# An attention block's backward pass: dWq and dWmod by whole rows through V's buffers

## The chip, the cores and the metric

The kernel runs on one core of a Trainium2 chip. The metric is the device time of one execution in microseconds; the median of three runs before the change is 1378.13 us (1377.52 to 1378.75).

The core has five engines that run at the same time: TensorE (PE) multiplies matrices into PSUM, VectorE (DVE) and ScalarE (ACT) do elementwise work and sums, GpSimd (POOL) and SyncE (SP) here mainly issue DMA transfers. Sixteen DMA engines move data between HBM and the on-chip SBUF, which has 128 partitions. A DMA transfer is split into packets; where a tile takes a contiguous run of bytes for each partition, the run is a packet.

## The reference

The reference computes one decode step of a transformer block (one token, D = 640, 32 heads of width 192, 8192 cached positions) and all of its gradients with respect to the inputs, the caches and most of the weights. Cut to what matters:

```python
mod = (silu(c) @ w_mod).reshape(1, 6, 1, 640)        # sa, ca, ga, sb, cb, gb
h = layernorm(x) * (1 + ca) + sa
q = (h @ wq).reshape(...)                            # wq: 640 x 6144
p = softmax(einsum(q, k) * 192 ** -0.5); o = einsum(p, v)
x = x + ga * (o @ wo)
h = layernorm(x) * (1 + cb) + sb
x = x + gb * B(h)                                    # a small MLP block
out, vjp = jax.vjp(f, x, k_cache, v_cache, wq, wo, w3, w4, c, w_mod)
grads = vjp(grad_out)
```

All arrays are bf16. The caches are 32 x 8192 x 192, so K, V, dK and dV are 100.7 MB each. The forward pass reads K and V, the backward pass reads V again and writes dK and dV. Two of the smaller gradients are the subject here. With dq (6144 values) and the input ha of the projection (640 values), dWq is the outer product ha x dq (640 x 6144), and the gradient of ha is Wq times dq, which sums each row of Wq weighted with dq. In the same way dWmod = silu(c) x dmod (640 x 3840), and Wmod times dmod goes into the gradient of c.

## The kernel before

A head's K or V is held as two tiles of 128 partitions x 32 positions x 192 values: 12,288 contiguous bytes for each partition, 1.5 MiB in all. The forward pass goes through the heads with a buffer set of its own. The backward pass runs in the order of heads HS (31 down to 0), in a loop over `i` (L1251) that emits, for each head:

- the side jobs of list `J0[i]`;
- `bwd_mult` for both halves: VectorE multiplies V by the broadcast gradient (L132), TensorE sums the products with an identity matrix into PSUM (L1018). From iteration 21 on this is done one head ahead;
- `ring_load` (L751): loads of V for later heads;
- for the next head, dV: ScalarE writes 20 of 32 positions of each half (L1023, one instruction each), VectorE the other 12 (L1001); stores on SyncE's queue (L1026);
- the side jobs of list `J1[i]`, then dS (`bwd_ds`) and dK for both halves on VectorE (L1001), with stores on SyncE's queue (L1053);
- the side jobs of list `J2[i]`.

So an iteration moves two tiles of V in, and two of dV and two of dK out: 9.44 MB. Each engine works in the order in which the program was written (`pin_order` fixes it for TensorE, VectorE and ScalarE); SyncE issues transfers in program order too, and a transfer whose data or buffer isn't ready holds all that are behind it. The program gives SyncE's transfers eight semaphores in turn, so at most eight of them are under way.

Buffers: dV and dK take tiles from `big`, five tiles in turn (`big_order`), and from iteration 25 (`I_SIDE` = 24) seven, with two tiles x and y that lie where the side jobs' pools were. V lives in a ring of six slots (`NR`), filled in the order of the list `ring`: two halves per head, and four batches of Wo early on. The load of entry n is emitted when entry n - 6 has been consumed.

The side jobs touched by the change compute dWq, dWmod and the two weighted row sums. Before, Wq is cut into four pieces of 1536 columns (`QG`) and Wmod into three of 1280 (`MG`), by `add_outer`; each piece takes two iterations:

- `job_outer_load` (L1114) loads all 640 rows of a piece, as 128 partitions x 5 blocks x 1536 or 1280 columns, on SyncE's queue;
- `job_outer_bc` broadcasts the piece of dq or dmod to all partitions: TensorE multiplies with the identity, four blocks of 128 at a time (L191), ScalarE copies from PSUM (L195);
- `job_outer_mul` multiplies on VectorE (L132) and sums on TensorE into 5 x 96 or 5 x 80 columns of PSUM with 16 matmuls (L1129);
- `job_outer_red` finishes the sum on VectorE (L1134 to L1138);
- `job_outer_out`, once for each of five row blocks, scales the broadcast by a column (`tsc`: ScalarE for even blocks, L1068, VectorE for odd ones, L1070) and stores 128 x 1536 or 128 x 1280 on SyncE's queue (L1143).

Wq's pieces are loaded at iterations 9, 11, 13, 15 and worked two iterations later, Wmod's at 17, 19, 21. `job_x0` (iteration 18) turns the finished sum into dx and into the first two parts of dmod, and `job_c` (iteration 24) makes the gradient of c. Their pools are `in` (one buffer), `out` (four) and `bc` (one).

Of the kernel before, what the change touches and what calls it, by code (L numbers as in the profile page):

```python
# [20 lines left out]
def kernel(  # L21
# [26 lines left out]
    nc = tc.nc  # L48
# [45 lines left out]
    def bank(tag, bufs=1, name=None, n=512):  # L94
        return psum[0].tile([P, n], FP32, tag=tag, name=name or "ps_" + tag, bufs=bufs)
# [35 lines left out]
    def mul(out, a, b):  # L131
        nc.vector.tensor_tensor(out=out, in0=a, in1=b, op=ALU.mult)  # L132

    def add(out, a, b):
        nc.vector.tensor_tensor(out=out, in0=a, in1=b, op=ALU.add)
# [50 lines left out]
    def bcast_cols(col_bf, c0, n, out_bc, evac, ps_in=None):  # L186
        for g0 in range(0, n, 4):
            g1 = min(n, g0 + 4)
            ps = ps_in if ps_in is not None else bank_c("bc_ps")
            for k in range(g0, g1):  # L190
                nc.tensor.matmul(ps[:, (k - g0) * P : (k - g0 + 1) * P], lhsT=col_bf[:, c0 + k : c0 + k + 1].to_broadcast([P, P]), rhs=ident_bf, start=True, stop=True)  # L191
            evac(out_bc[:, g0 * P : g1 * P], ps[:, 0 : (g1 - g0) * P])
# [135 lines left out]
    def load_v(pool, h, t, slot, eng=None):  # L328
        tl = pool.tile([P, JH, DH], BF16, name="V_sb", tag=f"v{slot}")
        (eng or nc.sync).dma_start(out=tl, in_=V_hd[h][:, t * JH : (t + 1) * JH, :])  # L330
        return tl
# [196 lines left out]
    def flat(tl):  # L528
        return tl.rearrange("p j d -> p (j d)")
# [206 lines left out]
    wo_b = {}  # L736
    WS = 32
    BATCHES = [(2, 3, 4), (5, 6, 7), (8, 9, 10), (11, 12, 13), (14, 15)]
    ring = []
    for i in range(1, HQ):  # L740
        ring += [("v", HS[i], t) for t in range(2) if (i, t) != (1, 1)]
        if i % 2 == 1 and 0 < i // 2 < len(BATCHES):
            ring.append(("w", i // 2, 0))
    ring_n, freed = [0], set()
    ldq = nc.sync
    NR = 6
# [4 lines left out]
    def ring_load():  # L751
        while ring_n[0] < len(ring) and (ring_n[0] < 3 or ring_key(ring_n[0] - NR) in freed):
            n = ring_n[0]
            kind, k, t = ring[n]
            slot = ring_slot(n)
            pool = bv if slot > 2 else fv
            ring_n[0] += 1
            if kind == "v":
                V_b.setdefault(k, {})[t] = load_v(pool, k, t, slot, ldq if n >= 3 else nc.sync)
            else:  # L760
                load_wo(k, pool.tile([P, JH, DH], BF16, name="V_sb", tag=f"v{slot}"))

    def load_wo(k, tl):
        lo, n = PS[BATCHES[k][-1]], len(BATCHES[k])
        tl = tl.rearrange("p j d -> p (j d)")[:, 0 : 3 * n * D].rearrange("p (c r) -> p c r", r=D)
        wo_b[k] = tl
        nc.gpsimd.dma_start(out=tl, in_=wo_v[:, 3 * lo : 3 * (lo + n), :])
# [341 lines left out]
    dha_c = ccol(NDC, "dha_c")  # L1109
    dsc_c = ccol(NDC, "dsc_c")  # L1110

    def job_outer_load(name, view, lo, n):
        w = side["in"].tile([P, NDC, n], BF16, name=name, tag="win")
        ldq.dma_start(out=w, in_=view[:, :, lo : lo + n])  # L1114
        side[name, lo] = w

    def job_outer_bc(name, lo, n, col_bf):
        v_bc = side["bc"].tile([P, n], BF16, name=name + "_bc", tag="vbc")
        bcast_cols(col_bf, lo // P, n // P, v_bc, act_copy)
        side[name + "_bc"] = v_bc  # L1120

    def job_outer_mul(name, lo, n):
        w = side.pop((name, lo))
        mul(w, w, side[name + "_bc"][:, None, :].to_broadcast([P, NDC, n]))
        ps = bank("b", name="js_ps")
        NS = 16
        W = n // NS
        for k in range(NS):
            nc.tensor.matmul(ps[:, 0 : NDC * W].rearrange("p (i w) -> p i w", w=W), lhsT=ident_bf, rhs=w[:, :, k * W : (k + 1) * W], start=(k == 0), stop=(k == NS - 1))  # L1129
        side[name + "_ps"] = ps[:, 0 : NDC * W].rearrange("p (i w) -> p i w", w=W)  # L1130

    def job_outer_red(name, acc, first):
        if first:
            nc.vector.reduce_sum(out=acc, in_=side[name + "_ps"], axis=AX.X)  # L1134
        else:
            red = bsm.tile([P, NDC], FP32, name="red")
            nc.vector.reduce_sum(out=red, in_=side[name + "_ps"], axis=AX.X)
            add(acc, acc, red)  # L1138

    def job_outer_out(name, lo, n, i, rows_f, dram):  # L1140
        o = side["out"].tile([P, n], BF16, name=name + "_o", tag="wout")
        tsc(o, side[name + "_bc"], rows_f[:, i : i + 1], i)
        st2.dma_start(out=dram[i * P : (i + 1) * P, lo : lo + n], in_=o)  # L1143

    def job_x0():
        dmod_sa, dmod_ca = dmod_c[:, 0:NDC], dmod_c[:, NDC : 2 * NDC]
# [14 lines left out]
        mul(sp, sp, dsc_c)  # L1161
        store_cols(out_8[0], sp, const, st2, "dco")

    QG = QD // 4
    MG = NMOD // 3
    NPH = 10
    J0, J1, J2 = [{i: [] for i in range(HQ)} for _ in range(3)]
    for k in range(HH):
# [3 lines left out]
    for k in range(NDC):  # L1172
        J1[5 + HH + k].append(lambda i=k: job_dw3(i))

    def add_outer(at, name, view, lo, n, col_bf, rows_f, dram, acc, first):
        J2[at].append(lambda: job_outer_load(name, view, lo, n))
        J0[at + 2].append(lambda: job_outer_bc(name, lo, n, col_bf))
        J1[at + 2].append(lambda: job_outer_mul(name, lo, n))
        J2[at + 2].insert(0, lambda: job_outer_red(name, acc, first))
        for i in range(NDC):  # L1180
            (J2[at + 2] if i < 3 else J1[at + 3]).append(lambda i=i: job_outer_out(name, lo, n, i, rows_f, dram))

    for g in range(4):
        add_outer(NPH - 1 + 2 * g, "wq", wq_v, g * QG, QG, dq_bf, ha_f, out_4, dha_c, g == 0)
    for k, g in enumerate((1, 2, 0)):
        add_outer(NPH + 7 + 2 * k, "wm", wm_v, g * MG, MG, dmod_bf, sc_f, out_9, dsc_c, k == 0)
    J2[NPH + 8].append(job_x0)
    J2[NPH + 14].append(job_c)

    wo_first = [(PS[1], cc) for cc in range(3)]  # L1190
# [60 lines left out]
    for i in range(HQ):  # L1251
        h, nxt = HS[i], HS[i + 1] if i + 1 < HQ else None
        if i % 2 == 1 and i > NPH and nxt is not None:
            bwd_dob(nxt // 2)
        for f in J0[i]:
            f()
        if i <= AHEAD:
            if i in SPLIT:
                bwd_pf(nxt)
            for t in range(2):  # L1260
                bwd_mult(h, t, 2 if i == 0 else 1)
                if i == t == 0:
                    ring_load()
                    c_first = fin_c(PS[0], 1)
                if i in SPLIT:
                    bwd_dv(nxt, t)
        if i not in EARLY:
            ring_load()
        if i - 1 in dq:
            fin_dq(*dq.pop(i - 1))  # L1270
        if i == 0:
            fin_c_copy(PS[0], 1, c_first)
        if nxt is not None and i not in SPLIT:
            if i > 0:
                bwd_pf(nxt)
            for t in range(0 if i > 0 else 1, 2):
                bwd_dv(nxt, t)
        if i in EARLY:
            ring_load()
        if i == 0:  # L1280
            bwd_ds(h)
            dq_last(h)
        if i < NPH:
            hook(i)
        if i == 3:
            bcast_cols(du_bf, 0, NFC, du_bc, act_copy)
        for f in J1[i]:
            f()
        if i > 0:
            bwd_ds(h)  # L1290
        if i >= AHEAD and nxt is not None:
            for t in range(2):
                bwd_mult(nxt, t)
        bwd_dk(h, 0)
        bwd_dk(h, 1)
        if i in cps:
            fin_c_copy(*cps.pop(i))
        if i == 1:
            mid_cols()
            job_mid()  # L1300
            dve_copy(dmod_bf[:, 2 * NDC : 6 * NDC], dmod_c[:, 2 * NDC : 6 * NDC])
        if i == NPH - 1:
            fin_dq(*dq.pop(i))
            mm_cm.__exit__(None, None, None)
            for nm, b in (("in", 1), ("out", 4), ("bc", 1)):
                side_cm.append(tc.tile_pool(name="side" + nm, bufs=b, side="right", reuse_waits="tile"))
                side[nm] = side_cm[-1].__enter__()
        for f in J2[i]:
            f()
        if i == I_SIDE:  # L1310
            while side_cm:
                side_cm.pop().__exit__(None, None, None)
            xt = ctx.enter_context(tc.tile_pool(name="xt", bufs=1, side="right", reuse_waits="tile"))
            for k in "xy":
                tail_tiles[k] = (xt, "xt" + k)
            for n in range(len(ring) - NR, len(ring)):
                slot = ring_slot(n)
                tail_tiles[f"v{n - len(ring) + NR}"] = (bv if slot > 2 else fv, f"v{slot}")
            big_order[:] = tail_list(big_order[0:5] + ["x", "y"])
    pin_order(first_ins)  # L1320


# [28 lines left out]
```

## Time and profile before

One execution was profiled: it took 1380.06 us, and the span from its first to its last instruction is 1378.3 us.

| | |
|---|---|
| median of three runs | 1378.13 us (1377.52 to 1378.75) |
| profiled execution, its span | 1380.06 us, 1378.3 us |
| bytes moved by DMA | 569.26 MB in 71,758 packets |
| busy: PE, DVE, ACT, POOL | 874.9, 1055.2, 946.0, 21.5 us |
| DMA queue 1 (SyncE), 0 (POOL) | 96.0%, 3.0% of 16 engines' span |
| backward loop | from about 577 us to the end |
| loads of Wq pieces | four of 1920 KB, issued at 812.8, 871.6, 928.6, 985.0 us |
| loads of Wmod pieces | three of 1600 KB, issued at 1041.3, 1097.7, 1155.4 us |
| stores of dWq, dWmod pieces | 20 of 384 KB, 15 of 320 KB |
| side products on VectorE | 4150 ns (Wq piece), 3485 ns (Wmod piece) |
| output scalings | ScalarE 1562 and 1347 ns, VectorE 612 and 546 ns |

A row of the costliest groups names line, engine and operation, tiles and shapes, the count, then the busy time in us and the mean in ns, and the idle time before with what ended it. A row of waits gives the waiting engine, its tile and line, what it waited for, the total in us, the number of times and the longest. In the DMA view each queue has its packets, its MB, and the time of its packets as a share of 16 engines over the stretch; packets are counted below 512 B, 2 KB and 8 KB, each count including the smaller ones. The digits of a slice are tenths.

### The profile page before, as it was taken

To read this page: it belongs to the slowest core of one execution; us is meant where nothing else is said; L and a number is where in the kernel's file an instruction comes from. 1 tells how busy PE (TensorE), PEld (TensorE's weight loads), DVE (VectorE), ACT (ScalarE), POOL (GpSimd) and SP (SyncE) were. 2 spreads that over 40 slices of the span, in tenths; PEclk is the share of its full clock that TensorE was granted. 3 is DMA by queue.
4 is the path that set the end of the run, shared out by engine and by line. 5 is a ranking of instruction groups with operands and counts; after the bars stand their busy time and mean duration, and the time that the engine had idled before them with its cause. 6 is when DMAs were issued, how large, how long until landed. Compare 5 with 4: busy or idle time off the path is not lost.

```text
span 1378.3 us, 28492 instructions
## 1 busy us (share of the span) xinstructions
PE 874.9 (63%) x11755; PEld 687.6 (50%) x11755; DVE 1055.2 (77%) x1199; ACT 946.0 (69%) x2586; POOL 21.5 (2%) x33
## 2 busy tenths in 40 slices
PE   3799999999999989747756653432334325324440
PEld 3577777777777777736635542322223213213330
DVE  3588778788878886899977776865867669679792
ACT  1388777778878884886866766766777676757770
POOL 0000000000000000000000000000000000000000
PEclk9999999999999998576676676776666767656665
DMA  9999999999999999899999999999999999999997
GB/s 393 415 416 420 418 418 420 421 413 421 416 407 420 417 419 362 318 394 425 422 419 427 423 427 423 421 428 422 424 425 422 427 420 417 425 425 420 428 427 316
DMA packets 71758, 569.26 MB, mean 413 GB/s; under 512 B 6796, under 2 KB 14476, under 8 KB 31436
## 3 DMA queue, kind: packets, MB, share of 16 engines
q1 hardware_dynamic: 67934, 550.73, 96.0%
q0 software_dynamic: 3664, 16.71, 3.0%
q8 instruction: 92, 1.51, 0.4%
q14 instruction: 38, 0.31, 0.1%
q10 hardware_dynamic: 30, 0.00, 0.0%
HBM read 341.51 MB, written 225.91 MB: 412 GB/s over the span
## 4 chain that ended last, share of the span: by engine, by line
DMA 43%; DVE 25%; PE 21%; ACT 5%; issue 2%; SPq 1%; DVEq 0%; ACTq 0%
DMA out_dram<-dV 24%; DMA K_sb<-in_A_k_cache_dram 8%; DVE prod L132 8%; DMA out_dram<-dK 7%; PE ps_a L432 7%; DVE dK L1001 6%; DVE V_sb L132 5%; PE S_ps L372 4%; ACT EK L407 3%; PE ps_b L443 2%; PE dP_ps L1018 2%; PE kb_ps L449 2%; DVE dV L1001 2%; DMA V_sb<-in_A_v_cache_dram 2%; ACT dV L1023 2%; DMA out_dram<-dw 2%
## 5 line engine op out<-in xcount | busy, mean ns | idle before, releaser
L1023 ACT ACTIVATE dV<-do_pb,PF 128x192 bf16<-128x192 bf16 x1246 | 436.1, 440 | 162.8 <-DMA out_dram<-dV 118.4
L1018 PE MATMUL dP_ps<-V_sb,ident_bf 128*128 128x256 bf16 (+1 forms) x1584 | 233.9, 323 | 193.5 <-DVE V_sb L132 193.5
L407 ACT ACTIVATE EK<-K_sb,E_f 128x192 bf16<-128x192 bf16 x992 | 351.1, 442 | 4.2 <-PE kb_ps L302 2.9
L1018 PEld LDWEIGHTS <-ident_bf 128*128 128x128 bf16 x1584 | 181.7, 118 | 245.2 <-issue 102.3
L1001 DVE TENSOR_TENSOR dK<-dS,q_pb 128x6144 bf16<-128x6144 bf16 x64 | 213.1, 3355 | 22.7 <-DMA out_dram<-dK 13.4
L132 DVE TENSOR_TENSOR prod<-K_sb,q_pb 128x6144 bf16<-128x6144 bf16 x64 | 214.4, 3349 | 4.3 <-DMA K_sb<-in_A_k_cache_dram 4.2
L132 DVE TENSOR_TENSOR V_sb<-V_sb,do_pb 128x6144 bf16<-128x6144 bf16 (+1 forms) x66 | 212.3, 3254 | 0.0
L432 PE MATMUL ps_a<-EK,V_sb 128*128 128x193 bf16 x1984 | 194.2, 250 | 0.9 <-ACT EK L407 0.9
L1001 DVE TENSOR_TENSOR dV<-P2h,do_pb 128x2304 bf16<-128x2304 bf16 (+2 forms) x67 | 89.9, 1354 | 122.9 <-DMA out_dram<-dV 118.7
L432 PEld LDWEIGHTS <-V_sb 128*128 128x128 bf16 x1984 | 166.9, 99 | 18.7 <-issue 12.7
L414 DVE TENSOR_TENSOR EK<-K_sb,P2h 128x1536 bf16<-128x1536 bf16 x124 | 117.6, 949 | 0.0
L372 PE MATMUL S_ps<-prod,ident_bf 64*64 64x256 bf16 x3072 | 102.0, 281 | 11.4 <-DVE prod L132 11.4
L443 PE MATMUL ps_b<-EK,V_sb 128*64 128x193 bf16 x1984 | 109.1, 253 | 0.0
L372 PEld LDWEIGHTS <-ident_bf 64*64 64x64 bf16 x3072 | 86.9, 111 | 31.7 <-issue 27.3
L443 PEld LDWEIGHTS <-V_sb 128*64 128x64 bf16 x1984 | 81.8, 110 | 19.6 <-issue 15.9
L393 ACT ACTIVATE E_f<-sm_ps,negm 128x64 f32<-128x64 f32 x31 | 9.7, 314 | 106.0 <-DVE negm L391 106.0
L376 DVE TENSOR_REDUCE S<-S_ps 128x128 f32<-128x1024 f32 x32 | 39.2, 1224 | 49.0 <-PE S_ps L372 49.0
L1129 PEld LDWEIGHTS <-ident_bf 128*128 128x128 bf16 x112 | 14.6, 131 | 124.2 <-issue 121.7
L449 PE MATMUL kb_ps<-EK,hot_bf 128*32 128x384 bf16 x992 | 64.5, 337 | 0.0
L1129 PE MATMUL js_ps<-wq,ident_bf 128*128 128x480 bf16 x64 | 21.1, 506 | 54.8 <-DVE wq L132 54.8
L1129 PE MATMUL js_ps<-wm,ident_bf 128*128 128x400 bf16 x48 | 14.6, 488 | 49.9 <-DVE wm L132 49.9
L1068 ACT ACTIVATE dwo<-dao_bc,o_col_f 128x640 bf16<-128x640 bf16 x48 | 36.1, 816 | 0.0
(262 smaller groups left out, 736.5 us busy)
## 6 DMA issues: line engine op xcount, KB each, us to landing
V_sb<-in_A_v_cache_dram SPq DMA_DIRECT2D x125, 1536.0 KB, 15.5
K_sb<-in_A_k_cache_dram SPq DMA_DIRECT2D x64, 1536.0 KB, 14.4
out_dram<-dK SPq DMA_DIRECT2D x64, 1536.0 KB, 23.9
out_dram<-dV SPq DMA_DIRECT2D x61, 1536.0 KB, 22.5
wq<-in_A_wq_dram SPq DMA_DIRECT2D x3, 2560.0 KB, 31.3
wo_t<-in_A_wo_dram SPq DMA_DIRECT2D x16, 480.0 KB, 15.6
out_dram<-dwo POOLq DMA_DIRECT2D x16, 480.0 KB, 9.0
wq<-in_A_wq_dram SPq DMA_DIRECT2D x4, 1920.0 KB, 24.0
```

The costliest lines, as they stand in the source:

```text
L132: nc.vector.tensor_tensor(out=out, in0=a, in1=b, op=ALU.mult)
L372: nc.tensor.matmul(st["S_ps"][c0 : c0 + 64, r, t * JH : (t + 1) * JH, :], lhsT=ident_bf[64 * r : 64 * r + 64, 64 * r : 64 * r + 64], rhs=p ...
L376: nc.vector.reduce_sum(out=st["S2"], in_=st["S_ps"], axis=AX.X)
L407: nc.scalar.activation(out=st["EK"][q][:, jj, 0:DH], in_=K_st[h, t][:, r * JQ + jj, :], func=ACT.Copy, scale=st["E_f"][:, j : j + 1])
L414: nc.vector.tensor_tensor(out=EK[:, NA:JQ, 0:DH].rearrange("p j (d r) -> p j d r", r=2), in0=K_st[h, t][:, r * JQ + NA : (r + 1) * JQ, :]. ...
L432: nc.tensor.matmul(st["A_ps"][:, 0:n], lhsT=V_sb[:, r * JQ + jj, a0:a1], rhs=EK[:, jj, 0:n], start=(q == 0 and jj == 0), stop=(q == 3 and ...
L443: nc.tensor.matmul(st["B_ps"][g : g + 64, 0:n], lhsT=V_sb[:, r * JQ + jj, b0:b1], rhs=EK[:, jj, 0:n], start=(q == 0 and jj < 2), stop=(q = ...
L449: nc.tensor.matmul(kb_ps[g : g + 32, 0 : 2 * DH], lhsT=hot_bf[:, HQ - 1 - h : 2 * HQ - 1 - h], rhs=EK[:, jj : jj + 2, 0:DH], start=(h == 0 ...
L1001: nc.vector.tensor_tensor(out=o.rearrange("p j (d r) -> p j d r", r=2), in0=pairs[:, :, None, :].to_broadcast([P, n, NP2, 2]), in1=vec.rea ...
L1018: nc.tensor.matmul(bst[h]["dP_ps"][:, t * JH + r : t * JH + r + n, :], lhsT=ident_bf, rhs=V_sb[:, :, k * DS : (k + 1) * DS], start=(k == 0 ...
L1023: nc.scalar.activation(out=o[:, jj, :], in_=vec_of(do_pb, h), func=ACT.Copy, scale=bst[h]["PF"][:, t * JH + jj : t * JH + jj + 1])
L1129: nc.tensor.matmul(ps[:, 0 : NDC * W].rearrange("p (i w) -> p i w", w=W), lhsT=ident_bf, rhs=w[:, :, k * W : (k + 1) * W], start=(k == 0), ...
```

## The change

Wq and Wmod are no longer cut by columns but by rows: five blocks of 128 whole rows each, 128 x 6144 and 128 x 3840. A block of Wq has the size of one half of V, and it is loaded into a slot of V's ring: the list `ring` gets one entry ("wq", u) after V's two entries for the iterations 11 to 15 (`Q_AT`), and ("wm", u) for 18 to 22 (`M_AT`). dq is broadcast whole (48 blocks, in two halves at iterations 10 and 11) and dmod whole (30 blocks, iterations 17 and 18) into one tile. For each block VectorE multiplies, TensorE sums into 512 or 480 columns of PSUM, VectorE reduces these to one column of the result; VectorE alone makes the output block, which is stored by whole rows. The pools are now `out` (two tiles of 6144 columns) and `bcp` (one), and since they are larger, three tiles x, y, z of the tail fit where they were: the tail turns over eight tiles. `job_x0` moves from iteration 18 to 16. The computed values are the same outer products and sums.

```diff
+    Q_AT, M_AT = 11, 18
+    SIDE_W = {"wq": A_wq, "wm": w_mod}
     ring = []
     for i in range(1, HQ):
         ring += [("v", HS[i], t) for t in range(2) if (i, t) != (1, 1)]
         if i % 2 == 1 and 0 < i // 2 < len(BATCHES):
             ring.append(("w", i // 2, 0))
+        for name, at in (("wq", Q_AT), ("wm", M_AT)):
+            if at <= i < at + NDC:
+                ring.append((name, i - at, 0))
...
+            elif kind == "w":
+                load_wo(k, pool.tile([P, JH, DH], BF16, name="V_sb", tag=f"v{slot}"))
             else:
-                load_wo(k, pool.tile([P, JH, DH], BF16, name="V_sb", tag=f"v{slot}"))
+                load_side(kind, k, pool.tile([P, JH, DH], BF16, name="V_sb", tag=f"v{slot}"))
...
+    def load_side(name, u, tl):
+        src = SIDE_W[name]
+        w = flat(tl)[:, 0 : src.shape[1]]
+        nc.sync.dma_start(out=w, in_=src[u * P : (u + 1) * P, :])
+        side[name, u] = w
+
+    def job_side_bc(name, lo, n, col_bf):
+        if lo == 0:
+            side["bc"] = side["bcp"].tile([P, JH * DH], BF16, name=name + "_bc", tag="vbc")
+        bcast_cols(col_bf, lo, n, side["bc"][:, lo * P : (lo + n) * P], act_copy)
+
+    def job_side_mul(name, u):
+        w = side.pop((name, u))
+        n = w.shape[1]
+        mul(w, w, side["bc"][:, 0:n])
+        m = 512 if n % 512 == 0 else 480
+        ps = bank("b", name="js_ps")[:, 0:m]
+        for k in range(n // m):
+            nc.tensor.matmul(ps, lhsT=ident_bf, rhs=w[:, k * m : (k + 1) * m], start=(k == 0), stop=(k == n // m - 1))
+        side["ps"] = ps
+        freed.add((name, u, 0))
+
+    def job_side_out(name, u, acc, rows_f, dram):
+        nc.vector.reduce_sum(out=acc[:, u : u + 1], in_=side["ps"], axis=AX.X)
+        n = dram.shape[1]
         o = side["out"].tile([P, n], BF16, name=name + "_o", tag="wout")
-        tsc(o, side[name + "_bc"], rows_f[:, i : i + 1], i)
-        st2.dma_start(out=dram[i * P : (i + 1) * P, lo : lo + n], in_=o)
+        nc.vector.tensor_scalar(out=o, in0=side["bc"][:, 0:n], scalar1=rows_f[:, u : u + 1], scalar2=None, op0=ALU.mult)
+        st2.dma_start(out=dram[u * P : (u + 1) * P, :], in_=o)
...
-    for g in range(4):
-        add_outer(NPH - 1 + 2 * g, "wq", wq_v, g * QG, QG, dq_bf, ha_f, out_4, dha_c, g == 0)
-    for k, g in enumerate((1, 2, 0)):
-        add_outer(NPH + 7 + 2 * k, "wm", wm_v, g * MG, MG, dmod_bf, sc_f, out_9, dsc_c, k == 0)
-    J2[NPH + 8].append(job_x0)
+    for lo in (0, NQC // 2):
+        J0[Q_AT - 1 + 2 * lo // NQC].append(lambda lo=lo: job_side_bc("wq", lo, NQC // 2, dq_bf))
+    for lo in (0, NMC // 2):
+        J0[M_AT - 1 + 2 * lo // NMC].append(lambda lo=lo: job_side_bc("wm", lo, NMC // 2, dmod_bf))
+    for u in range(NDC):
+        J1[Q_AT + u].append(lambda u=u: job_side_mul("wq", u))
+        J2[Q_AT + u].append(lambda u=u: job_side_out("wq", u, dha_c, ha_f, out_4))
+        J1[M_AT + u].append(lambda u=u: job_side_mul("wm", u))
+        J2[M_AT + u].append(lambda u=u: job_side_out("wm", u, dsc_c, sc_f, out_9))
+    J2[Q_AT + NDC].append(job_x0)
...
-            for nm, b in (("in", 1), ("out", 4), ("bc", 1)):
+            for nm, b in (("out", 2), ("bcp", 1)):
...
-            for k in "xy":
+            for k in "xyz":
...
-            big_order[:] = tail_list(big_order[0:5] + ["x", "y"])
+            big_order[:] = tail_list(big_order[0:5] + ["x", "y", "z"])
```

More of the change, by code (lines that the diff above doesn't have):

```diff
@@ L1110 @@
     dsc_c = ccol(NDC, "dsc_c")
[L1112 to L1140, printed above, removed]
+    def load_side(name, u, tl):
[3 more added lines that the diff above has]
+        side[name, u] = w
@@ L1162, in job_c @@
         store_cols(out_8[0], sp, const, st2, "dco")
-    QG = QD // 4
-    MG = NMOD // 3
     NPH = 10
@@ L1173 @@
         J1[5 + HH + k].append(lambda i=k: job_dw3(i))
[L1175 to L1181, printed above, removed]
-    for g in range(4):
-        add_outer(NPH - 1 + 2 * g, "wq", wq_v, g * QG, QG, dq_bf, ha_f, out_4, dha_c, g == 0)
-    for k, g in enumerate((1, 2, 0)):
-        add_outer(NPH + 7 + 2 * k, "wm", wm_v, g * MG, MG, dmod_bf, sc_f, out_9, dsc_c, k == 0)
-    J2[NPH + 8].append(job_x0)
+    for lo in (0, NQC // 2):
[8 more added lines that the diff above has]
+    J2[Q_AT + NDC].append(job_x0)
     J2[NPH + 14].append(job_c)
```

## The prediction

> **What bounds the kernel now.** I read the page first: its slices and its DMA rows.
>
> ```profile
> DMA  9999999999999999899999999999999999999997
> GB/s 393 415 416 420 418 418 420 421 413 421 416 407 420 417 419 362 318 394 425 422 419 427 423 427 423 421 428 422 424 425 422 427 420 417 425 425 420 428 427 316
> ...
> q1 hardware_dynamic: 67934, 550.73, 96.0%
> q0 software_dynamic: 3664, 16.71, 3.0%
> ```
>
> All 16 DMA engines are busy in every slice except around 520 to 600 us, where the backward pass starts, and in the drain at the end. VectorE, the busiest compute engine, is at 77%. The chain of waits names many engines, but between 600 and 1350 us its long steps are stores of dV and dK.
>
> Then I read the table of stretches for the part that holds the edited jobs (812 to 1210 us), and beside it a later part with whole tiles alone. After the engines' busy times the last two columns are DMA share and GB/s.
>
> ```profile
> 812.00:1210.00 398.00, 152.52 (x956) 106.98 (x956) 288.20 (x188) 270.75 (x671) 8.38 (x11) 0.68 1.01 423
> 1250.00:1350.00 100.00, 38.77 (x252) 29.64 (x252) 91.71 (x50) 72.05 (x208) 0.00 (x0) 0.69 1.01 427
> ```
>
> The DMA share is 1.01 in both (records of packets overlap a little). VectorE (288.2 of 398) and ScalarE (270.8) have more than 100 us to spare in the first. The waits of that stretch say what they spare it for:
>
> ```profile
> DVE dV L1001 <- DMA out_dram<-dV: 94.6, 13, 12.7
> ACT dV L1023 <- DMA out_dram<-dV: 85.7, 14, 9.7
> ```
>
> They wait for buffers whose stores still stand in the queue. A store of dV there lands 22.2 us after its issue in the median, one of dK 23.4, and the shortest of all 16.6, although 1.5 MiB at 423 GB/s takes 3.7. So the time is bytes over rate, and a change of compute is worth nothing while the queue stays full. The bytes don't change. What can change is the time that an engine needs per packet, so I priced packets, from the DMA view of stretches with different mixes.
>
> Stretch 1280 to 1350, whole tiles (rows of 12,288 B):
>
> ```profile
> DMA packets 2737, 29.91 MB, mean 427 GB/s; under 512 B 303, under 2 KB 303, under 8 KB 303
> ...
> q1 hardware_dynamic: 2734, 29.87, 100.7%
> q8 instruction: 2, 0.03, 0.2%
> ```
>
> 100.7% of 16 x 70 us is 1127.8 engine-us for 2734 - 303 = 2431 rows (the 303 are completion words): 463.9 ns a row.
>
> Stretch 812 to 1041, with wq in pieces of 1536 columns (3072 B):
>
> ```profile
> DMA packets 12987, 97.12 MB, mean 424 GB/s; under 512 B 1251, under 2 KB 1251, under 8 KB 6540
> ...
> q1 hardware_dynamic: 12024, 92.86, 96.6%
> q0 software_dynamic: 953, 4.14, 4.4%
> ```
>
> Over 8 KB there are 12987 - 6540 = 6447 packets, less 10 of the instruction queues: 6437 rows. They take 6437 x 463.9 = 2986 of 0.966 x 16 x 229 = 3539 engine-us. The other 553 belong to (92.86 - 79.10) MB / 3072 = 4480 packets: 123.5 ns each, 494 for 12,288 B, or 6.5% more than one row.
>
> Stretch 1100 to 1150, with wm in pieces of 1280 columns (2560 B):
>
> ```profile
> DMA packets 3086, 21.24 MB, mean 425 GB/s; under 512 B 288, under 2 KB 288, under 8 KB 1664
> ...
> q1 hardware_dynamic: 2972, 20.73, 98.9%
> q0 software_dynamic: 112, 0.49, 2.5%
> ```
>
> In the same way: 1420 rows take 658.7 of 791.2, and 1280 packets share 132.5: 103.5 ns each.
>
> Stretch 5 to 12, at the start, where w_mod is loaded by whole rows of 7680 B:
>
> ```profile
> DMA packets 459, 3.00 MB, mean 428 GB/s; under 512 B 69, under 2 KB 69, under 8 KB 459
> ...
> q1 hardware_dynamic: 441, 3.00, 101.9%
> ```
>
> 390 packets in 1.019 x 16 x 7 = 114.1 engine-us: 292.6 ns a row, where three pieces of 2560 B take 310.5.
>
> **The change, part by part.**
>
> *Loads and stores by whole rows.* wq is 7.86 MB loaded and 7.86 stored: 5120 packets x 123.5 = 632.3 engine-us before, 1280 x 463.9 = 593.8 after; 38.5 less, over 16 engines 2.4 us. wm: 3840 x 103.5 = 397.4 before, 1280 x 292.6 = 374.5 after; 22.9 less, 1.4 us. Together 3.8 us of engine time. Small packets also overlap more: the queues' shares sum to 101.2% in 812 to 1041 (and in 1041 to 1210 too), to 100.9% in 1280 to 1350. If that excess goes with the pieces, 0.3% of 398 us, 1.2 us, is given back: 2.6. Between 2.6 and 3.8 I take the middle, 3.2, as nothing in the rows favours an end. The 42 side transfers become 20, so 22 x 16 completion words fall away; no row prices one, it is inside the figures above, and I put it at nothing.
>
> [...]
>
> *Loads in V's ring.* A load of wq or wm takes a slot of the six and its place in SyncE's order: in the iterations 11 to 15 and 18 to 22 that order is wq (or wm), V, V, dV, dV, dK, dK, one store. V is then fetched two iterations ahead, not three. An iteration there moves 9.44 + 3.15 + 0.49 MB, at 423 GB/s 30.9 us (two take 56.4 before), so V has some 60 us against a landing of 18.2 to 26.9. A slot is freed by TensorE's reads of the row block one iteration earlier. Cost: nothing, covered by the queue. POOL issues the same transfers in the same order.
>
> *Compute.* ScalarE loses its 21 output scalings (12 x 1.56 + 9 x 1.35 = 31 us). VectorE takes all ten: from 612 ns at 1536 columns and 546 at 1280, a block of 6144 costs between 1.8 (that slope) and 2.45 (four times). In iterations 11 to 15 VectorE gets 3.35 (product, as V's) + 0.65 (sum, as now) + 2.45 = 6.5 us on top of 16.8 (39.8 for the two iterations from 985 to 1041.3, less 6.2 of side work, halved): 23.3 of 30.9. In 18 to 22 it is 2.15 (a product of 3840 columns) + 0.65 + 1.6 on 16.8, or 21.2 of 28. Covered. TensorE's sums go from 112 matmuls of 480 and 400 columns to 100 of 512 and 480.
>
> *The broadcasts.* Six groups of four blocks instead of three stand ahead of the products at iterations 10, 11 (wq), and four at 17, 18 (wm). One group costs ScalarE 0.585 us, with two PSUM banks 0.65 in the row: at most 6 x 0.65 = 3.9 us by which TensorE reads V later; next late are the slots' release and the V loads queued on SyncE, with dV behind them. Covered by the queue: the shortest landing, 16.6, holds 10 us that is neither the transfer (3.7) nor the 2.8 that a lone 768 KB store needs beyond its bytes (4.7 - 1.9). If the cover were gone: 2 x 3.9 + 2 x 2.6 = 13 us. The column work for dx0 moves from iteration 18 to 16, just ahead of the first wm broadcast, which reads its result: some ten small VectorE operations (35 in the two iterations from 1041.3, against 24 in the two before), 0.17 us each, delay TensorE by about 2 us. Covered in the same way.
>
> *Pools and tail.* Two tiles of 12,288 B for outputs: one is rewritten two iterations (60 us) after its store was queued. From iteration 24 stores turn over eight buffers, not seven; compute would wait less, but the queue is full to beyond 1360 us, so nothing. The last transfer ends where the bytes do.
>
> Sum: the profiled execution took 1380.06 us (span 1378.3, 1.8 around it); 1380.06 - 3.2 = 1376.9. The median of the runs lies 1.93 lower, at 1378.13: **1374.9 us**.
>
> **Rivals.**
> *A, the forecast*: the queue stays full, 1374.9, alone from 1373.7 to 1376.1.
> *B, packet size hardly counts*: the 6% belongs to mixing small transfers among large, not to their packets. For it: the lone stretch with 7680 B rows has no stores beside it, so its price may not carry over. Against: the line through 3072 B (123.5) and 12,288 B (463.9) gives 293.7 at 7680 B, where that stretch has 292.6. Half the gain or none: 1376.5 to 1378.1. [...]
> *C, slower: the queue runs dry at the broadcasts and the shallower ring*. For it: VectorE's work grows by a sixth (19.9 to 23.3 an iteration) and V's lead shrinks by an iteration, while all loads stand in one order. It decides once a wait on SyncE passes some 10 us; the longest wait of SyncE for VectorE or TensorE in this part is now 8.2. Price: 13 us uncovered, less 3.2: 1378.13 + 9.8 = 1387.9; partly covered, from 1381 on.
> *D, each transfer costs the engines a fixed gap*: with the 2.8 us above, 22 fewer save 62 us: 1316. Against: the share of 1.01 leaves no such gaps.
> [...]
>
> **How the numbers follow.** A 0.79, B 0.06, C 0.14, D 0.01. A measurement of this kernel can tell about 0.2%, 2.8 us, from no change; A's centre of 3.2 lies just beyond it, so of its 0.79 I count 0.57 as faster and 0.22 as the same. With D: faster 0.58; with B: same 0.28; C: slower 0.14. The range runs from 1371.9 (3.8 us, 1.2 more if whole rows overlap more instead of less, and 1.2 for the spread of the runs, off 1378.13) to 1378.8 (no gain, and the 0.6 by which the slowest run lies above the median): it takes in B and leaves C and D out.
>
> **What would show it.** Right: DMA share 1.01 in every stretch from 600 to 1350, packets under 8 KB fewer by 5120 + 2560 net (7680 B rows still count there), GB/s of 812 to 1210 nearer 427, landings still above 16 us, the last store some 3 us earlier. Wrong: a slice below 1.00 after 812 us (C), and then SyncE's waits name the instruction; or the same shares and rates with fewer packets (B).

## The result, and the profile after

The changed kernel takes 1374.51 us (median of 21 runs, 1373.04 to 1376.30), the kernel before, run beside it, 1376.73 (21 runs, 1375.84 to 1378.83). The medians differ by 2.2 us. The ratio of the runs is 0.998, or 2.8 us less, with a 95% interval from 0.9974 to 0.9986, or 1.9 to 3.6 us less. The forecast was 3.2 us less and 1374.9.

The page of the changed kernel: its GB/s in 40 slices, its packets and SyncE's queue.

```profile
GB/s 392 412 413 420 420 419 419 419 412 414 418 409 421 419 407 387 336 394 424 423 419 426 424 424 427 422 428 425 428 425 424 427 427 428 426 428 427 428 429 309
DMA packets 65006, 569.26 MB, mean 414 GB/s; under 512 B 6444, under 2 KB 14124, under 8 KB 23404
...
q1 hardware_dynamic: 61182, 550.73, 96.1%
```

The bytes are the same, 569.26 MB. Below 8 KB there were 31,436 packets and are 23,404: 8032 fewer, which are the 5120 + 2560 pieces of the forecast and 22 x 16 = 352 completion words (6796 packets below 512 B before, 6444 now). From the 24th slice (790 us) to the last but one the rate no longer dips below 422 (417 before); the last is the drain at the end.

The table of stretches, for the two that were shown of before (the last two columns are DMA share and GB/s):

```profile
812.00:1210.00 398.00, 162.71 (x936) 107.90 (x935) 294.51 (x176) 246.67 (x663) 8.39 (x11) 0.66 1.01 426
1250.00:1350.00 100.00, 37.33 (x252) 28.58 (x252) 90.23 (x48) 67.25 (x194) 0.00 (x0) 0.68 1.01 429
```

The share is still 1.01; the rate rose from 423 to 426 GB/s. Not all of such a rise need be the change: from 1250 to 1350 us both kernels move the same packets, and there it rose from 427 to 429. VectorE works 6 us more, ScalarE 24 less. The waits of 812 to 1210 have the same owners:

```profile
ACT dV L1030 <- DMA out_dram<-dV: 111.1, 14, 13.5
DVE dV L1008 <- DMA out_dram<-dV: 93.4, 14, 11.8
```

The shortest landing (from issue to arrival) of a dV or dK store or of a load into V's ring there is 16.9 us (16.6 before): the queue stayed full. SyncE's longest wait there for a compute engine is 6.7 us, for VectorE's dK:

```profile
SPq L1060 <- DVE dK L1008: 43.4, 22, 6.7
```

And the DMA view of 812 to 1041:

```profile
DMA packets 9576, 97.45 MB, mean 426 GB/s; under 512 B 1101, under 2 KB 1101, under 8 KB 2125
...
q1 hardware_dynamic: 8670, 93.41, 96.6%
q0 software_dynamic: 896, 3.93, 4.2%
```

SyncE's queue fills the same 96.6% as before with 12,024 - 8670 = 3354 packets fewer, and in that time moved 0.55 MB more.

The profiled executions differ by 4.9 us in span (1378.3 and 1373.4), twice the difference of the medians. The bytes moved in each stretch tell which part of that is the change:

| stretch, us | MB before | MB after | lead of after at 424 GB/s, us |
|---|---|---|---|
| 0 to 500 | 207.69 | 207.14 | -1.3 |
| 500 to 620 | 43.99 | 45.40 | +3.3 |
| 620 to 812 | 81.35 | 81.30 | -0.1 |
| 812 to 1041 | 97.12 | 97.45 | +0.8 |
| 1041 to 1210 | 71.36 | 72.04 | +1.6 |
| 1210 to 1241 | 13.15 | 13.27 | +0.3 |
| 1241 to 1350 | 46.37 | 46.73 | +0.8 |

Up to 500 us and around the start of the backward loop (500 to 620) the instructions are the same in both, yet the lead moves by -1.3 and +3.3 us: one execution differs from the next by that much. After 1241 us, when the last pieces of the old kernel are stored, the packets are the same again, and the lead still grows by 0.8. The edited part, 812 to 1241, makes +2.7 us in this pair, between the 2.2 of the medians and the 2.8 of the ratio.

### The profile page after: what moved, and what is told of

It reads as the page before. It is cut to its first block, busy times and chain, and to the rows that moved or that the text cites. A ratio compares the mean times of both kernels' runs of the same rounds, so it can differ in the third digit from the quotient of the medians.

```text
span 1373.4 us, 28399 instructions
## 1 busy us (share of the span) xinstructions
PE 881.4 (64%) x11743; PEld 686.0 (50%) x11743; DVE 1062.8 (77%) x1196; ACT 916.5 (67%) x2564; POOL 21.5 (2%) x33
## 2 busy tenths in 40 slices
DMA packets 65006, 569.26 MB, mean 414 GB/s; under 512 B 6444, under 2 KB 14124, under 8 KB 23404
## 4 chain that ended last, share of the span: by engine, by line
DMA 38%; DVE 28%; PE 23%; ACT 4%; SPq 2%; issue 2%; DVEq 0%; ACTq 0%
DMA out_dram<-dV 25%; DVE prod L132 9%; PE ps_a L432 8%; DVE dK L1008 6%; DMA out_dram<-dK 6%; DVE V_sb L132 6%; PE S_ps L372 4%; DMA V_sb<-in_A_v_cache_dram 3%; PE dP_ps L1025 3%; PE ps_b L443 3%; PE kb_ps L449 2%; DVE dV L1008 2%; DMA K_sb<-in_A_k_cache_dram 2%; ACT dV L1030 2%; ACT EK L407 2%
## 5 line engine op out<-in xcount | busy, mean ns | idle before, releaser
L1025 PE MATMUL dP_ps<-V_sb,ident_bf 128*128 128x256 bf16 (+1 forms) x1584 | 237.0, 326 | 203.8 <-DVE V_sb L132 203.5
L1008 DVE TENSOR_TENSOR dK<-dS,q_pb 128x6144 bf16<-128x6144 bf16 x64 | 212.6, 3354 | 15.7 <-DMA out_dram<-dK 12.0
L372 PE MATMUL S_ps<-prod,ident_bf 64*64 64x256 bf16 x3072 | 98.8, 275 | 11.4 <-DVE prod L132 11.4
L1137 PE MATMUL js_ps<-V_sb,ident_bf 128*128 128x512 bf16 (+1 forms) x100 | 40.7, 587 | 88.8 <-DVE V_sb L132 88.8
L195 ACT CAST do_pb<-bc_ps 128x384 bf16<-128x384 f32 x15 | 7.1, 470 | 51.1 <-PE bc_ps L191 51.1
```

Of the source, the lines that this page charges most:

```text
L372: nc.tensor.matmul(st["S_ps"][c0 : c0 + 64, r, t * JH : (t + 1) * JH, :], lhsT=ident_bf[64 * r : 64 * r + 64, 64 * r : 64 * r + 64], rhs=p ...
L1008: nc.vector.tensor_tensor(out=o.rearrange("p j (d r) -> p j d r", r=2), in0=pairs[:, :, None, :].to_broadcast([P, n, NP2, 2]), in1=vec.rea ...
L1025: nc.tensor.matmul(bst[h]["dP_ps"][:, t * JH + r : t * JH + r + n, :], lhsT=ident_bf, rhs=V_sb[:, :, k * DS : (k + 1) * DS], start=(k == 0 ...
L1137: nc.tensor.matmul(ps, lhsT=ident_bf, rhs=w[:, k * m : (k + 1) * m], start=(k == 0), stop=(k == n // m - 1))
```

## Experiments

Each run was timed beside the kernel before on one chip. The last column takes the difference of the ratios to the kernel before, times 1377 us, with the two intervals combined.

| run | median, us | ratio to before | against the changed kernel, us |
|---|---|---|---|
| packets of 3072 and 1920 B | 1377.82 | 1.0005 (0.9996 to 1.0014) | +3.4 ± 1.5 |
| packets of 768 and 960 B | 1392.09 | 1.0109 (1.0096 to 1.0123) | +17.8 ± 2.0 |
| small packets in the loads alone | 1385.91 | 1.0060 (1.0040 to 1.0080) | +11.0 ± 2.9 |
| small packets in the stores alone | 1386.34 | 1.0064 (1.0049 to 1.0079) | +11.6 ± 2.2 |
| halves of 64 rows | 1415.39 | 1.0277 (1.0263 to 1.0292) | +40.9 ± 2.2 |
| quarters of 32 rows | 1422.32 | 1.0327 (1.0292 to 1.0362) | +47.8 ± 4.9 |
| Wo of the forward pass by GpSimd | 1375.44 | 0.9985 (0.9976 to 0.9994) | +0.7 ± 1.5 |
| scaling written six times | 1376.69 | 0.9993 (0.9983 to 1.0002) | +1.8 ± 1.5 |
| scaling written eleven times | 1419.52 | 1.0306 (1.0291 to 1.0322) | +44.9 ± 2.3 |
| broadcasts not halved | 1375.43 | 0.9988 (0.9979 to 0.9998) | +1.1 ± 1.5 |
| seven tail buffers | 1374.04 | 0.9974 (0.9965 to 0.9983) | -0.8 ± 1.5 |

### Is it the packets?

Two transfers for each block, each with every second piece of all rows, keep everything of the change but the packet size (shown with two pieces in each transfer; `b` is 2 here):

```diff
-        nc.sync.dma_start(out=w, in_=src[u * P : (u + 1) * P, :])
+        for a in range(2):
+            nc.sync.dma_start(out=w.rearrange("p (b a n) -> p a b n", a=2, b=b)[:, a], in_=src[u * P : (u + 1) * P, :].rearrange("p (b a n) -> p a b n", a=2, b=b)[:, a])
...
-        st2.dma_start(out=dram[u * P : (u + 1) * P, :], in_=o)
+        for a in range(2):
+            st2.dma_start(out=dram[u * P : (u + 1) * P, :].rearrange("p (b a n) -> p a b n", a=2, b=b)[:, a], in_=o.rearrange("p (b a n) -> p a b n", a=2, b=b)[:, a])
```

> The changed kernel with each row block still in one V slot and one output tile, but moved as two transfers of interleaved pieces, so that its packets are 3072 B (wq) and 1920 B (wm). My theory, that a packet costs 10 ns beside its bytes (the line through 123.5 ns at 3072 B and 463.9 ns at 12,288 B): 3 more packets for each of 2560 rows, 76.8 engine-us, +4.8 us against the changed kernel, 1379.3 us, some 2.6 above the kernel before. [...] If the gain came from the ring, the broadcasts or the tail and not from packets: no difference, 1374.5.

With `b` = 8 for wq and 4 for wm:

> As the run with pieces, with 768 B (wq) and 960 B (wm) packets: 15 more packets for each of 1280 rows and 7 more for each of 1280, 28,160 packets. Theory of 10 ns a packet: +17.6 us against the changed kernel, 1392 us, with a DMA share of 1.01 throughout. [...] Not packets: 1374.5.

Cutting the rows into pieces again undoes the gain: the run takes 1.0005 of the kernel before (0.6 us less to 1.9 more, where my price of 10 ns had 2.6 more). It is 3.4 us above the changed kernel; my 4.8 lies just inside its interval, 1.9 to 4.9. With small packets it is 17.8 us, where 10 ns a packet gave 17.6. From one run to the other the number of transfers is the same (40) and 20,480 packets are added: 14.3 us x 16 / 20,480 = 11 ns for each. In both runs, as in the kernel before, the pieces of one transfer lie apart in HBM; no run separates that from their number. The DMA view of the run with small packets, 1041 to 1210:

```profile
DMA packets 15551, 69.71 MB, mean 412 GB/s; under 512 B 985, under 2 KB 10180, under 8 KB 10820
...
q1 hardware_dynamic: 15094, 67.64, 98.9%
q0 software_dynamic: 448, 1.97, 2.9%
```

The share is as full as ever, 98.9 + 2.9%, and the rate is 412 where the changed kernel has 426: the engines' time is full, and it moves fewer bytes.

The price of a packet is not one number, though. The change itself took 6400 packets of data away (8960 became 2560), so its 2.2 to 2.8 us are 5.5 to 7 ns for each (4.7 to 9 by the interval), and the run with 3072 and 1920 B gives 7 (4 to 10). Only the small packets show 10 and more.

Then the small packets in one direction alone:

> The changed kernel with small packets (768 B for wq, 960 B for wm) in the loads alone, 14,080 packets more. The run with both cost 17.8 us more than the changed kernel (ratios 1.0109 and 0.998). If a packet costs the same in both directions: +8.9 us, 1383.4. If only one direction counts: +17.8 or 0.

> The same in the stores alone, 14,080 packets more: +8.9 us, 1383.4, if both directions cost the same; the two runs together should make 17.8.

Both directions pay, about equally (11.0 and 11.6), but each more than the 8.9 expected; the stores' 11.6 ± 2.2 excludes it. Their sum, 22.6, is 4.8 above the 17.8 of both together, just beyond the 4.0 that the intervals allow. That small packets in both directions overlap each other would fit: from 812 to 1250 us the shares of the queues 1 and 0 sum to 100.8% in the changed kernel, 101.0 and 101.1 with one direction and 101.9 with both. The 0.6% that is more than the two parts together is 2.6 us of the 4.8; the rest stays open.

### Is it the number of transfers?

```diff
-        nc.sync.dma_start(out=w, in_=src[u * P : (u + 1) * P, :])
+        for g in (0, 64):
+            nc.sync.dma_start(out=w[g : g + 64], in_=src[u * P + g : u * P + g + 64, :])
```

and the stores in the same way.

> The changed kernel with each row block moved as two transfers of 64 whole rows: twice the transfers (40 instead of 20), the same packets. Packet theory: 1374.5, within 0.5 us. [...]

This missed by far: 40.9 us more with the same packets. The table of stretches of that run, four pieces of 10 us:

```profile
880.00:890.00 10.00, 1.95 (x10) 0.81 (x8) 10.00 (x5) 7.26 (x19) 0.76 (x1) 0.67 0.99 332
890.00:900.00 10.00, 7.69 (x48) 5.87 (x49) 5.13 (x4) 2.60 (x8) 0.00 (x0) 0.74 1.00 358
907.00:917.00 10.00, 1.83 (x4) 0.69 (x5) 6.67 (x5) 6.68 (x20) 0.00 (x0) 0.50 1.01 410
917.00:927.00 10.00, 2.69 (x8) 0.83 (x6) 10.00 (x5) 6.13 (x15) 0.76 (x1) 0.67 1.00 279
```

All DMA engines are busy (share 0.99 to 1.01), but at times the rate falls to 279 GB/s: packets take longer while halves pass. So it is not a gap between transfers, which at the prediction's 2.8 us would have made 56 us for 20 more, and the runs above with 40 transfers of all 128 partitions don't show it (the first of them costs 3.4 us). The next expectation counts from the kernel before (38 us); from the changed kernel it is the 40.9 of the table. Quarters tell whether the rate goes with the number of partitions:

> The halves of 64 rows cost 38 us though their packets were those of the changed kernel. Here each row block moves as four transfers of 32 whole rows (80 transfers instead of 20). Theory 1, a transfer that covers fewer partitions runs at a lower rate, in proportion: quarters run at half the rate of the halves, and the loss grows from 38 us to some 100 (1475 us). Theory 2, a transfer of 32 partitions can use as much as one of 64: the loss stays near 38 us (1412 us). Theory 3, a fixed cost of each added transfer (38 us for 20): 60 added ones cost 114 us (1489 us).

Quarters cost 47.8 us (two runs, 8 us apart), 7 more than halves: 60 added transfers where there were 20, and half the partitions in each, change little. The second theory comes nearest (38 us against the kernel before, measured 45.0), with no cause shown; the first and third, at some 100 and 114, are out. Rival D of the prediction, a fixed gap, falls too: 20 more transfers of whole width cost 3.4 us with 7680 more packets among them.

### What the cover is worth

VectorE's output scaling repeated, for wq alone:

```diff
+        for _ in range(6 if name == "wq" else 1):
-        nc.vector.tensor_scalar(out=o, in0=side["bc"][:, 0:n], scalar1=rows_f[:, u : u + 1], scalar2=None, op0=ALU.mult)
+            nc.vector.tensor_scalar(out=o, in0=side["bc"][:, 0:n], scalar1=rows_f[:, u : u + 1], scalar2=None, op0=ALU.mult)
```

> The changed kernel with the output scaling of each wq block written six times instead of once on VectorE: 5 x 1.81 = 9.0 us more in each of the iterations 11 to 15, where VectorE now works 24.1 of 30.9 us. VectorE then needs 33.1 us an iteration, 2.2 more than the transfers, 11 us over the five. Theory that the queue covers it (some 20 us of transfers are always outstanding): no change, 1374.5, within 2 us. Theory that there is no cover: +11 us, 1385.5.

> The same with eleven scalings instead of one: 18.1 us more, VectorE 42.2 us an iteration against 30.9, 56 us over the five iterations. Cover theory: the queue takes the first 10 to 20 us, so +36 to +46 us, 1411 to 1421, with a DMA share below 1.00 in the later iterations and SyncE waiting for VectorE. No cover: +56, 1431. If VectorE's own idle time counts for nothing (it waits elsewhere too): more.

With six, 46 us of added VectorE work cost 1.8 ± 1.5 us. The stretches of that run:

```profile
862.00:912.00 50.00, 19.64 (x113) 13.43 (x114) 49.58 (x27) 28.90 (x77) 1.52 (x2) 0.63 1.01 427
912.00:962.00 50.00, 13.20 (x76) 8.31 (x77) 49.47 (x29) 23.83 (x65) 0.76 (x1) 0.67 1.01 426
962.00:1012.00 50.00, 19.33 (x107) 12.92 (x108) 47.56 (x27) 24.57 (x65) 1.53 (x2) 0.67 1.01 411
```

VectorE is busy 49.5 of 50 us, and the DMA share doesn't move; only the rate dips to 411 in the third stretch, for a reason that no run tested. From 812 to 1062 the median landing of a store falls from 24.4 us in the changed kernel to 18.1, which is the queue being eaten. SyncE's longest wait is for the scaling:

```profile
SPq L1147 <- DVE wq_o L1146: 56.0, 5, 11.2
```

With eleven the queue runs dry:

```profile
862.00:912.00 50.00, 10.59 (x65) 7.18 (x65) 49.40 (x27) 27.07 (x73) 0.76 (x1) 0.60 0.93 379
912.00:962.00 50.00, 10.18 (x59) 6.83 (x60) 49.40 (x28) 17.39 (x46) 2.90 (x2) 0.60 0.72 277
```

and SyncE's longest wait from 812 to 1062 is again for the scaling:

```profile
SPq L1147 <- DVE wq_o L1146: 101.0, 5, 20.5
```

The scalings of the blocks start 31.85 us apart with six and 41.13 with eleven, with VectorE hardly ever idle. So an iteration needs 22.6 us of VectorE in the changed kernel (31.85 less the 9.28 of five added scalings), not the 24.1 that both expectations took, and what was added goes beyond the transfers' 30.7 by 1.2 and 10.4 us, or 6 and 52 over the five, not 11 and 56. Of the 52 us, 44.9 show in the time.

The run with eleven also shows how long a full queue lasts. Ahead of the first scaling SyncE issues its last transfer at 857.9 us and the next at 878.5; the DMA share is still 0.99 from 870 to 875 and falls to 0.39 from 875 to 880. That is about 17 us, the shortest landing. The prediction let rival C decide from a wait of SyncE of some 10 us; the 11.2 us of the run with six left no gap in the DMA share, and the point lies nearer 17. The changed kernel, with 6.7, stays clear of it.

The broadcasts in one piece, `J0[Q_AT - 1]` and `J0[M_AT - 1]` for both halves:

> The changed kernel with all 48 blocks of dq broadcast ahead of the products of iteration 10 and all 30 of dmod ahead of those of iteration 17, instead of in halves: 12 groups (7.8 us) and 8 groups (5.2 us) in a row. Cover theory: no change, 1374.5, within 1 us. If the broadcasts lie on the path: about +4 to +13 us.

+1.1 ± 1.5 us: not told from no change, and all of 4 to 13 is excluded. The tail with seven buffers (`"xy"` instead of `"xyz"`):

> The changed kernel with seven buffers in the tail, as before, not eight (z is left out). Queue theory: no change, 1374.5, within 1 us. If the third tile feeds the tail: slower by some us.

No difference is seen (-0.8 ± 1.5): the third tile of the tail gains nothing that the runs can tell.

### Can the same rule win elsewhere?

```diff
-            nc.sync.dma_start(out=st["wo"], in_=wo_v[:, c0 : c0 + 3, :])
+            nc.gpsimd.dma_start(out=st["wo"], in_=wo_v[:, c0 : c0 + 3, :])
```

> The changed kernel with the 16 loads of Wo in the forward pass issued by GpSimd instead of SyncE. On GpSimd's queue rows of 1280 B go as packets of 5120 B, 199 ns each; on SyncE's queue as 1280 B, by the line 57.3 ns, 229 for four. Packet theory: 1536 x 30 ns over 16 engines, 2.9 us less, 1371.6 us. If the forward pass is not bound by packets, or GpSimd issues late: 1374.5 or more.

A miss: +0.7 ± 1.5 instead of -2.9. The DMA view of 100 to 500, first of the changed kernel, then of this run:

```profile
DMA packets 19846, 166.60 MB, mean 416 GB/s; under 512 B 1830, under 2 KB 6822, under 8 KB 6822
...
q1 hardware_dynamic: 19779, 165.61, 99.8%
```

```profile
DMA packets 16129, 166.89 MB, mean 417 GB/s; under 512 B 1833, under 2 KB 1833, under 8 KB 3081
...
q1 hardware_dynamic: 14605, 159.50, 95.6%
q0 software_dynamic: 1456, 6.39, 4.1%
```

4992 packets of 1280 B have become 1248 of 5120 B. The 4.1% of 16 x 400 us for those (6.39 MB / 5120) are 262 engine-us, 210 ns each, not the 199 I took from the backward pass; SyncE's queue gave back 4.2%, 54 ns for each packet of 1280 B, not the 57.3 of the line. Both prices were off by some 6%, and the forecast was the small difference between them: four times 54 is 215, next to 210. The stretch moved 0.29 MB more, 0.7 us, less than two executions differ. It isn't shown either that the transfers alone bound this stretch: TensorE is busy 381 of its 400 us. On GpSimd's queue a packet held four rows (5120 B), so that one run of bytes is one packet, as said of transfers at the start, held in these runs for SyncE's queue alone. None of the runs beats the changed kernel by more than its interval.

## Why the prediction was right, point by point

- *The bound.* Right. The share is 1.01 in every stretch read between 600 and 1350 us in both kernels, and repeated VectorE work costs next to nothing until it has eaten the queue.
- *The packet term.* The mechanism is right: cutting the rows undoes the gain, cutting them finer costs 17.8 us of a forecast 17.6. The size, 3.2 us, was somewhat too large: measured were 2.2 by the medians, 2.8 by the ratio (1.9 to 3.6) and 2.7 by the bytes of the edited stretches in one pair of profiles. The forecast lies in the interval, in its upper half. Of its two ends (2.6 and 3.8 us) the lower one, with the overlap of small packets given back, was the better, and the upper one lies outside. The shares show a part of that overlap: before they sum to 101.2% in 812 to 1041 and in 1041 to 1210, in the changed kernel to 101.0 and 100.9. The second of these is, beside 0.1 and 0.1 for the instruction queues:

```profile
q1 hardware_dynamic: 7186, 70.47, 98.6%
q0 software_dynamic: 336, 1.47, 2.1%
```

- *The time itself.* That 1374.9 came within 0.4 us of 1374.51 is in part luck: the sum started from 1378.13, and beside the changed kernel the old one took 1376.73. The gain was 0.4 to 1.0 us smaller than forecast, and the start 1.4 lower.
- *V's ring.* Right: two iterations of lead were enough. An iteration took 30.7 us (SyncE's dK stores issued at 908.6 and 939.3), forecast 30.9, and the longest landing in the ring was 30.7 us, against some 60 of lead.
- *Compute.* Right, and with less on VectorE than feared: the scaling of 6144 columns takes 1.81 us, the lower of my two values. VectorE is busy 22.6 us in each of the two iterations from 908.6 to 970.05 (forecast 23.3, with 2.45 for the scaling).
- *The broadcasts.* Right to cost them at nothing; even whole they cost 1.1 ± 1.5.
- *Pools and tail.* Right: without the third tile the time is the same within 1.5 us.
- *The rivals.* B falls with the runs of cut rows. C's mechanism exists, as the eleven scalings show, but sets in far from here, and later than the 10 us that the prediction gave it. D falls: the halves that seemed to show it keep the engines busy (share 0.99 to 1.01), and quarters, with three times as many added transfers, cost 7 us more instead of some 80. The completion words, put at nothing, are priced by no run.

## What to carry to other kernels

Where the DMA engines are busy throughout, as here, packets can be priced: take from stretches of different mixes what a packet of each size costs, and multiply by the packets that a change removes. Here that came within 0.4 to 1.0 us of the gain; for the loads on GpSimd's queue it failed, as the difference of two prices is no better than the prices. Before the difference of two profiles is believed, compare the bytes moved stretch by stretch: of the 4.9 us between this pair, only some 2.7 lay where the kernels differ. And in this kernel the row blocks were best moved 128 partitions wide: 64 cost 40.9 us more, 32 cost 47.8.

## What was not expected of the hardware

Transfers of 64 partitions were slow although all 16 engines were busy: moving 25.6 MB in halves cost 40.9 us on top of the 60 us that they take at 424 GB/s, and in quarters 47.8. That is 0.68 and 0.79 of those 60 us: halving the width once more added only 7 us. Why is not shown: transfers of all 128 partitions ran beside the halves and quarters, and no run moved these alone.

The price of a packet, 5.5 to 7 ns beside its bytes by the change itself, was enough to tell 12,288 B rows from 3072 B ones, and with 768 and 960 B packets it was 10 to 13 (11.6 us x 16 for 14,080 packets of the stores).
